# Softmax sums inverted on ten columns, the two halves of the attention output copied by ScalarE and added per head pair, and new numbers in the planner

## The chip, the cores and the metric

One core of a Trainium2 chip runs one program. Its engines are TensorE (PE; its weight loads are shown apart as PEld), VectorE (DVE), ScalarE (ACT), GpSimd (POOL) and SyncE (SP), which here only issues DMAs. The metric is the device time of one run in microseconds, from the first to the last instruction and what little lies around it.

## What is computed

Three layers in fp32, for 4 x 576 = 2304 tokens. Only the first is touched by the change.

```python
# attention: 4 batches, 8 heads, 576 positions, head size 64
scores = scale * q @ k.T + (cum[:, :, :, None] - cum[:, :, None, :])   # cum: running sum of log f
scores = where(causal, -1e9, scores); scores -= max(scores)
attn = exp(scores)
attn = attn / (sum(attn, axis=-1, keepdims=True) + 1e-09)
x = concat_heads(attn @ v)                                             # 2304 x 512
# first MLP
h = (x @ w1) * (x @ w2) @ w3;  x = h @ w_out
# second MLP
xn = x / rms(x) * rms_g;  y = (silu(xn @ w_gate) * (xn @ w_val)) @ w_out
```

## The kernel before

Most products run as three fp32r passes: a tensor is split into a rounded high part and the rest (two instructions: a copy with rounding and a subtraction), and high x high, high x low and low x high are added in PSUM.

**A planner sets all orders.** The program adds operations to a list with `plan.op([(engine, ns, lock), ...], ...)`. An operation can name several engines. `Plan.order()` then lays the operations out in time with the costs written in the code (`t_dve`, `t_act`, `t_pool`, `pe`), due times worked back from the dates that TensorE's operations carry (`S0`, `TE`, `T1`, `LT`, `LP`, `FD`, `FR`), the factor `WAIT`, and lags between engines that are longer in the middle of the program (`MARGIN`, `MARGIN2`). What it gives is the fixed order of each engine's queue, and the engine of each operation that had a choice. On the chip each engine works through its queue in order and waits for semaphores.

**Attention** takes 32 heads, two heads (p = 0, 1) to a pair. For one head: TensorE makes the scores (`attn_s`) in the PSUM tile `wide` and in two of the tiles `bank0` to `bank2`; DVE takes row maxima (`row_max`, L429, tiles `PB`, `nmax`); ACT makes the exponentials and their sums (`row_exp`, L436, `rsum`); TensorE transposes the blocks (L471); ACT and DVE split them (L486 `PTh`, L487 `PTl`); TensorE multiplies with V (`pv`, L520, L526) back into `wide`. V's high and low parts lie side by side as 128 columns, so that `wide` then holds two halves, partitions 0 to 63 and 64 to 127, whose sum is the head's output. In `pv` ACT copies the lower half to `half` (which lies in the tile `rq0`, L530) and DVE adds it to the upper half (L531) into the tile `x`; then `wide` is free for the next head's scores.

**The sums.** Once per pair TensorE transposes the 128 x 10 sums to 10 x 128 (L477), DVE adds 1e-9 (L478) and inverts (L479) that row tile `rrow`, and two DMAs spread it as `rall`. `normalize` multiplies `x` by `rall` (L536, DVE or POOL).

**Weights.** Beside the attention of the first heads, weights are loaded as integers and split: `convert` rescales their high words on ACT (L549) and their low words on DVE (L550), DVE joins the two (L552), and `unit` splits (L254, L256 the copies, L247 the subtractions). Then `wc_group` multiplies w3 by w_out (L625), so that the first MLP needs one product less. The first MLP (`ab_group` L662, `y_group` L687) runs between the later heads, the second (L867, L948) after them.

Of the kernel before, what the change touches and what calls it, by code (L numbers as in the profile page):

```python
# [51 lines left out]

S0, TE, T1 = 0, 7500, 13700
LT, LP = 5000, 13000

WC0, WCP = 18000, 9400

FD, FR = 25000, 1.8

WAIT, SLIP = 2.0, 1200  # L60

DMA0, COLD, RS, RB = 2500, 7000, 230, 330
MT, MARGIN, MARGIN2 = 135000, 600, 300
MT2, MARGIN3 = 538000, 200
# [148 lines left out]
def body(ctx, tc, q, k, v, f, w12, w3, wo1, wgv, wo2, g, out):  # L213
# [9 lines left out]
    def pe(cols, fn, r=(), w=(), at=0, times=1):  # L223

        plan.op([("PE", times * (max(110, 0.4167 * cols + 13.4)), False)], lambda e, times=times: fn(), r, w, at)

    def t_dve(n, rate=1.04, lock=False):
        return "DVE", 70 + rate * n, lock

    def t_act(n, fixed=95):  # L230
        return "ACT", fixed + 0.833 * n, False

    def t_pool(n, rate=2.1):
        return "POOL", 170 + rate * n, True
# [14 lines left out]
    def copy(n, o, a, r=(), w=(), by=1.0):  # L249

        def run(e):
            o_, a_ = (x() if callable(x) else x for x in (o, a))
            if e == "ACT":
                A.activation(o_, a_, AF.Copy, scale=by)  # L254
            else:
                on[e].tensor_scalar(out=o_, in0=a_, scalar1=by, scalar2=1.0, op0=ALU.mult, op1=ALU.mult)  # L256

        plan.op([t_act(n), t_dve(n, 0.52, True), t_pool(n, 0.83)], run, r, w)

# [30 lines left out]
    g_sb = const.tile([P, KD], F32, name="g_sb")  # L290
    tok = const.tile([P, 3 * BW // P], F32, name="tok")
    trow = const.tile([BW // P, P], F32, name="trow")

    rq = [att.tile([P, S], F32, name=f"rq{i}") for i in range(2)]
    half = rq[0][D:P, :]
    rk = [att.tile([P, S], F32, name=f"rk{i}") for i in range(2)]
# [164 lines left out]
    def transpose(h, parts, o, key, pt, at):  # L461
# [35 lines left out]
    def pv(h, at):  # L497
        p, j, (b, pp) = h % 2, h % 2, divmod(h // 2, H // 2)
        t, wk = wide, ["wide"]
# [28 lines left out]
        pe(192, tail, [(a, c) for a in ("PTh", "PTl") for c in (PT_KB0, PT_KB3)] + [("V2", p), ("V2h", p)], wk, at, 2)  # L528
        x_to, x_key = X[b % 2][j * D:(j + 1) * D, pp, :], ["cq"] * (b == 0) + wk + [("x", b % 2, pp, j)] + [("raw", "x1")] * (b == 1)
        act(S, lambda: A.copy(half, t[D:P, 0:S]), [], ["half", ("nrowq", 0)] + wk, at, 180)  # L530
        dve(S + 100, lambda: V.tensor_add(x_to, t[0:D, 0:S], half), ["half"], x_key, at)  # L531

    def normalize(h, at):
        b, pp = divmod(h // 2, H // 2)
        x = X[b % 2][:, pp, :]
        plan.op([t_dve(S, lock=True), t_pool(S)], lambda e: on[e].tensor_mul(x, x, rall), [("rall", 0), ("rall", 1)], [("x", b % 2, pp, j) for j in range(2)])  # L536

    def convert(raw, key, src, at_load, r_load=(), w_load=(), to=None):
# [4 lines left out]
        def lo():  # L543
            return u32(raw()).rearrange("p (n t) -> p n t", t=2)[:, :, 0]
# [494 lines left out]
    def start():  # L1039
# [179 lines left out]
```

## Time and profile before

| | |
|---|---|
| median of 3 runs | 952.07 us (950.26 to 952.71) |
| profiled execution | 951.07 us, its span 949.3 us |
| PE busy | 934.7 us, 98% of the span |
| DVE busy | 814.3 us, 86% |
| ACT busy | 516.1 us, 54% |
| POOL busy | 227.7 us, 24% |

The span runs from the first to the last instruction; 1.8 us of the execution lie around it. Busy times are averages over stages with different limits. A PE that is busy has matmuls in flight, which need not follow each other at full rate. TensorE's granted clock is 1.0 throughout, the level of 2.4 GHz.

### The profile page before, as it was taken

How to read it: one execution, taken by the hardware profiler on the slowest of the kernel's cores; microseconds unless marked ns; L12 is line 12 of the kernel's file. 1: busy time of each engine (PE TensorE's matmuls, PEld its weight loads, DVE VectorE, ACT ScalarE, POOL GpSimd, SP SyncE). 2: the span in 40 equal slices, each digit the busy share in tenths (PEclk: the TensorE clock that was granted, in tenths of full speed). 3: DMA queues.
4: the chain of work that ended last, by engine and by line, in shares of the span. 5: the costliest groups of instructions: out<-in, count | busy, mean ns of one | idle time of the engine just before them, and what ended most of it. 6: DMA issues, size and time to landing. Idle time of an engine off the chain costs nothing.

```text
span 949.3 us, 15520 instructions
## 1 busy us (share of the span) xinstructions
PE 934.7 (98%) x5516; PEld 894.5 (94%) x5516; DVE 814.3 (86%) x1486; ACT 516.1 (54%) x1056; POOL 227.7 (24%) x238
## 2 busy tenths in 40 slices
PE   8999999999999999999999999999999999999998
PEld 4687789999999999999999999999999999999998
DVE  8999999989997999475664779989988899988896
ACT  6777777757775567433332245446445456444442
POOL 2155326454445334202010021115000012000000
PEclk9999999999999999999999999999999999999999
DMA  6964565456545643166876335422754324633422
GB/s 229 294 214 162 159 218 180 167 197 208 188 149 185 196 147 134 30 256 244 300 247 235 112 117 196 175 105 68 228 210 141 106 91 147 223 137 117 134 68 100
DMA packets 47697, 161.67 MB, mean 170 GB/s; under 512 B 5674, under 2 KB 22236, under 8 KB 40964
## 3 DMA queue, kind: packets, MB, share of 16 engines
q1 hardware_dynamic: 47620, 160.69, 49.9%
q8 instruction: 43, 0.70, 0.3%
q14 instruction: 34, 0.28, 0.1%
HBM read 130.13 MB, written 30.53 MB: 169 GB/s over the span
## 4 chain that ended last, share of the span: by engine, by line
PE 73%; DVE 12%; DMA 2%; issue 2%; ACT 0%; SPq 0%; DVEq 0%
PE bank L867 27%; PE bank L662 16%; PE bank L687 10%; PE bank L948 9%; PE wide L948 3%; PE bank L471 3%; PE wide L520 3%; DVE PTl L487 1%; DVE wbig L247 1%; DMA raw_w<-in_wgv 1%; PE bank L625 1%; DVE qk L247 1%; PE bank L413 1%; PE bank L412 1%; DVE lbig L247 1%
## 5 line engine op out<-in xcount | busy, mean ns | idle before, releaser
L662 PE MATMUL bank<-xhl,wbig 128*128 128x384 f32 x1152 | 216.3, 338 | 0.1
L662 PEld LDWEIGHTS bank<-xhl,wbig 128*128 128x128 f32 x1152 | 198.0, 188 | 1.9 <-DVE xhl L247 0.4
L867 PE MATMUL bank<-xop,wbig 128*128 128x384 f32 x1008 | 182.3, 335 | 0.6 <-ACT cs L889 0.5
L867 PEld LDWEIGHTS bank<-xop,wbig 128*128 128x128 f32 x1008 | 175.1, 188 | 1.5 <-ACT cs L889 0.8
L867 PE MATMUL bank<-xop,lbig 128*128 128x384 f32 x504 | 94.4, 334 | 0.0
L867 PEld LDWEIGHTS bank<-xop,lbig 128*128 128x128 f32 x504 | 88.0, 188 | 0.0
L486 ACT CAST PTh<-bank 128x512 fp32r<-128x512 f32 (+2 forms) x116 | 55.3, 506 | 25.9 <-PE bank L471 21.5
L487 DVE TENSOR_TENSOR PTl<-bank,PTh 128x512 fp32r<-128x512 f32 (+2 forms) x116 | 64.3, 576 | 4.7 <-ACT PTh L486 4.4
L687 PE MATMUL bank<-uh,Wch 128*128 128x384 f32 x192 | 65.2, 339 | 0.0
L687 PE MATMUL bank<-uh,Wcl 128*128 128x384 f32 x192 | 64.3, 335 | 0.0
L687 PE MATMUL bank<-ul,Wch 128*128 128x384 f32 x192 | 64.2, 335 | 0.0
L625 PE MATMUL bank<-wbig,w 128*128 128x512 f32 x192 | 53.4, 406 | 0.5 <-DVE wbig L247 0.5
L670 ACT CAST uh<-u 128x384 fp32r<-128x384 f32 x48 | 24.6, 515 | 49.5 <-DVE u L669 49.4
L669 DVE TENSOR_TENSOR u<-bank,a 128x384 f32<-128x384 f32 x48 | 26.4, 550 | 29.1 <-PE bank L662 27.7
L520 PE MATMUL wide<-PTl,V 128*128 128x512 f32 (+4 forms) x145 | 43.6, 327 | 2.3 <-DVE PTl L487 2.2
L247 DVE TENSOR_TENSOR lbig<-zf,lbig 128x768 fp32r<-128x768 f32 x46 | 44.6, 976 | 0.1
L520 PE MATMUL wide<-PTh,V 128*128 128x512 f32 (+4 forms) x145 | 44.4, 317 | 0.1
L247 DVE TENSOR_TENSOR wbig<-nrm,wbig 128x768 fp32r<-128x768 f32 (+1 forms) x41 | 43.8, 1071 | 0.3 <-ACT wbig L254 0.3
L873 DVE TENSOR_TENSOR zf<-cs 128x384 f32<-128x384 f32 x72 | 40.1, 557 | 4.3 <-ACT cs L878 2.3
L765 POOL TENSOR_TENSOR xf<-xf 128x768 f32<-128x768 f32 (+1 forms) x5 | 23.8, 4756 | 81.7 <-DVE xf L552 25.4
L254 ACT ACTIVATE lbig<-zf 128x768 fp32r<-128x768 f32 x32 | 27.2, 850 | 25.7 <-PE bank L948 9.6
L625 PEld LDWEIGHTS bank<-wbig,w 128*128 128x128 f32 x192 | 33.9, 189 | 6.6 <-DVE wbig L247 1.2
(285 smaller groups left out, 2218.8 us busy)
## 6 DMA issues: line engine op xcount, KB each, us to landing
xf<-sw_d SPq DMA_DIRECT2D x24, 896.0 KB
nrm<-sw_d SPq DMA_DIRECT2D x12, 896.0 KB
wbig<-w_d SPq DMA_DIRECT2D x10, 1024.0 KB
rk<-in_k SPq DMA_DIRECT2D x62, 144.0 KB
nrm<-wo_d SPq DMA_DIRECT2D x11, 768.0 KB
raw_w<-in_wgv SPq DMA_DIRECT2D x8, 1024.0 KB
xf<-wo_d SPq DMA_DIRECT2D x10, 768.0 KB
sw_d<-raw_w SPq DMA_DIRECT2D x8, 896.0 KB
```

Source lines behind the costliest of these rows:

```text
L247: plan.op([t_dve(n, lock=True), t_pool(n)], lambda e: on[e].tensor_sub(*(x() if callable(x) else x for x in (o, a, b_))), r, w)
L254: A.activation(o_, a_, AF.Copy, scale=by)
L471: T.transpose(o[:, c * P:(c + 1) * P], PB[p][i][:, kb * P:(kb + 1) * P], ident)
L486: act(n, lambda: A.copy(PTh[:, pt:pt + n], o[:, lo:lo + n]), [], [("PTh", pt), key], at, 55)
L487: dve(n, lambda: V.tensor_sub(PTl[:, pt:pt + n], o[:, lo:lo + n], f32(PTh[:, pt:pt + n])), [("PTh", pt)], [("PTl", pt), key], at)
L520: pe(w, lambda s_=s_, o=o, w=w, c=c, kb=kb, m=m, src=src: T.matmul(t[:, o:o + w], V2[p][:, kb, :], src[:, c:c + w], start=(s_ == 0 and m = ...
L625: T.matmul(o, a, b_, start=(ft == 0 and m == 0), stop=(ft == KF - 1 and m == 2))
L662: T.matmul(o, a, x[:, kt, :], start=(kt == 0 and i == 0), stop=(kt == KD - 1 and i == 2))
L687: T.matmul(o, a[:, es], x[:, ft, 0:w], start=(q == 0 and ft % 2 == 0 and i == 0), stop=(q == 3 and ft % 2 == 1 and i == 2))
L867: T.matmul(o, w[:, a, j, kt], x[c][:, kt], start=start and kt == 0 and i == 0, stop=kt == 1 and i == 2, skip_group_check=not start)
L873: plan.op([t_dve(TH, lock=True), t_pool(TH)], lambda e: on[e].tensor_mul(o(), x(), y()), r, w)
L948: T.matmul(tiles[m], wv[:, a, k, m], z[c][:, kt], start=start and k == 0 and x == 0, stop=k == KH - 1 and x == 2, skip_group_check=not start)
```

## The change

Four edits go together.

1. **Sums.** 1e-9 is added and the inverse taken on the 128 x 10 tile `rsum`, ahead of the transpose. What follows the transpose is a plain copy to `rrow`, on ACT or DVE.
2. **Halves.** ACT copies both halves out of `wide`: the upper to `x`, the lower to a new tile `xlow`. Once per pair `normalize` adds `xlow` to `x` on 128 partitions, on DVE or POOL, and then multiplies.
3. **Low words.** `convert` may also rescale low words on ACT, as a Prelu with a slope of 0 and a bias column `under`.
4. **Numbers.** POOL's costs in the planner go up, and dates, lags and the factor `WAIT` change.

```diff
-S0, TE, T1 = 0, 7500, 13700
+S0, TE, T1 = 0, 8000, 13200
-FD, FR = 25000, 1.8
+FD, FR = 20000, 1.9
-WAIT, SLIP = 2.0, 1200
+WAIT, SLIP = 4.0, 1200
-MT, MARGIN, MARGIN2 = 135000, 600, 300
+MT, MARGIN, MARGIN2 = 135000, 600, 700
...
-    def t_pool(n, rate=2.1):
-        return "POOL", 170 + rate * n, True
+    def t_pool(n, rate=2.5):
+        return "POOL", 190 + rate * n, True
...
-        plan.op([t_act(n), t_dve(n, 0.52, True), t_pool(n, 0.83)], run, r, w)
+        plan.op([t_act(n), t_dve(n, 0.52, True), t_pool(n, 0.95)], run, r, w)
...
-            pe(128, lambda: T.transpose(row, rsum[pr].rearrange("p j i -> p (j i)"), ident), [("rsum", pr, j, i) for j in range(2) for i in range(5)], [key], at)
-            dve(P, lambda: V.tensor_scalar_add(rrow, row, 1.0e-9), [], ["rrow", key], at)
-            dve(P, lambda: V.reciprocal(rrow, rrow), [], ["rrow"], at)
+            dve(80, lambda: V.tensor_scalar_add(sums, sums, 1.0e-9), [], keys, at)
+            dve(100, lambda: V.reciprocal(sums, sums), [], keys, at)
+            pe(128, lambda: T.transpose(row, sums, ident), keys, [key], at)
+            plan.op([t_act(P), t_dve(P, 1.6)], lambda e: (A.copy if e == "ACT" else V.tensor_copy)(rrow, row), [], ["rrow", key])
...
-        act(S, lambda: A.copy(half, t[D:P, 0:S]), [], ["half", ("nrowq", 0)] + wk, at, 180)
-        dve(S + 100, lambda: V.tensor_add(x_to, t[0:D, 0:S], half), ["half"], x_key, at)
+        act(S, lambda: A.copy(x_to, t[0:D, 0:S]), [], x_key + wk, at)
+        act(S, lambda: A.copy(low, t[D:P, 0:S]), [], [("xlow", j)] + wk, at)
...
+        if h - 1 >= NP:
+            plan.op([t_dve(S, lock=True), t_pool(S)], lambda e: on[e].tensor_add(x, x, low), [("xlow", j) for j in range(2)], keys)
+        elif h >= NP:
+            dve(S, lambda: V.tensor_add(x[D:], x[D:], low[D:]), [("xlow", 1)], keys[1:])
+        plan.op([t_dve(S, lock=True), t_pool(S)], lambda e: on[e].tensor_mul(x, x, rall), [("rall", 0), ("rall", 1)], keys)
...
-        dve(1024, lambda: V.tensor_scalar(out=lo(), in0=lo(), scalar1=2.0**-29, scalar2=7.0, op0=ALU.mult, op1=ALU.min), [key], [kl], rate=0.52, lock=True)
+        def bits(e):
+            if e == "ACT":
+                A.activation(lo(), lo(), AF.Prelu, scale=2.0**-29, bias=under, alpha=0.0)
+            else:
+                V.tensor_scalar(out=lo(), in0=lo(), scalar1=2.0**-29, scalar2=7.0, op0=ALU.mult, op1=ALU.min)
+
+        plan.op([t_act(1024), t_dve(1024, 0.52, True)], bits, [key, "under"], [kl])
```

How this moves the queues is seen at three places.

DVE's queue in the second batch's first pairs, before: the row tile is made from the transposed sums (L478), and after a weight subtraction, a row maximum and three subtractions it is inverted on 128 columns (L479).

```order
L669 TENSOR_TENSOR u_133<-bank_64,a_131 128x384
L478 TENSOR_SCALAR rrow<-bank_60 10x128
L247 TENSOR_TENSOR wbig<-nrm,wbig 128x1024
L429 ISA PB4a,nmaxa<-wide,mask 128x576
L429 ISA nmaxa 128x1
L487 TENSOR_TENSOR PTl<-bank_59,PTh 128x448
L487 TENSOR_TENSOR PTl<-bank_60,PTh 128x320
L487 TENSOR_TENSOR PTl<-bank_61,PTh 128x384
L479 RECIPROCAL rrow<-rrow 10x128
```

And in the change, some ten rows earlier in the same heads' work: the sums are inverted on ten columns (L480, L481) among subtractions of the first MLP (`ul`), which stood on POOL before.

```order
L247 TENSOR_TENSOR qk_106<-rq_100,qk_106 64x576
L247 TENSOR_TENSOR qk_106<-rk_102,qk_106 64x576
L247 TENSOR_TENSOR wbig<-raw_w_1286,wbig 128x1024
L480 TENSOR_SCALAR rsumb<-rsumb 128x10
L247 TENSOR_TENSOR ul<-u_134,uh 128x384
L481 RECIPROCAL rsumb<-rsumb 128x10
L247 TENSOR_TENSOR wbig<-nrm,wbig 128x1024
L247 TENSOR_TENSOR ul<-u_135,uh 128x384
```

The inversion now stands ahead of the transpose that TensorE makes of the sums; the additions L531 are gone from this queue.

ACT's queue at the end of a head of the second batch, before: one copy out of `wide` (L530), other work behind it.

```order
L254 ACTIVATE wbig<-raw_w_1282 128x1024
L530 COPY rq_100<-wide 64x576
L667 COPY a_131<-bank_63 128x384
L254 ACTIVATE V_107<-rv_104 128x5x64
L254 ACTIVATE wbig<-nrm 128x1024
L486 CAST PTh<-bank_61 128x512
```

In the change, with a low-word pass (first row) and two copies out of `wide`; a weight copy and a split stand between the two.

```order
L563 ACTIVATE nrm<-nrm,tok 128x1024
L684 COPY a_132<-bank_62 128x384
L254 ACTIVATE wbig<-raw_ul 128x1024
L535 COPY x_131<-wide 64x576
L254 ACTIVATE wbig<-nrm 128x1024
L490 CAST PTh<-bank_61 128x512
L536 COPY xlow<-wide 64x576
```

`wide` is now given back by the second of these copies and not by DVE.

POOL's queue in the second batch, before: splits of V and of k, and the first MLP's subtractions `ul`.

```order
L247 TENSOR_TENSOR V_108<-rv_105,V_108 128x5x64
L256 TENSOR_SCALAR qk_106<-rk_102 128x576
L247 TENSOR_TENSOR qk_106<-rk_102,qk_106 64x576
L247 TENSOR_TENSOR ul<-u_133,uh 128x384
L247 TENSOR_TENSOR V_107<-rv_104,V_107 128x5x64
L247 TENSOR_TENSOR ul<-u_134,uh 128x384
```

In the change: the additions of pairs (L543) have come in, the subtractions of k and most of `ul` have gone to DVE.

```order
L543 TENSOR_TENSOR x_131<-x_131,xlow 128x576
L546 TENSOR_TENSOR x_131<-x_131,rall 128x576
L256 TENSOR_SCALAR qk_106<-rk_102 128x576
L247 TENSOR_TENSOR V_107<-rv_104,V_107 128x5x64
L256 TENSOR_SCALAR qk_106<-rk_103 128x576
L247 TENSOR_TENSOR qk_106<-rq_101,qk_106 64x576
```

Over the whole program POOL's queue holds 218 rows before and 162 in the change, DVE's 1438 and 1480, ACT's 878 and 931. TensorE has the same instructions in another order.

## Rows read from the trace of the kernel before

**Rows 1.** The page: span

```profile
span 949.3 us, 15520 instructions
```

**Rows 2.** Busy time by stretch: PE, PEld, DVE, ACT, POOL, clock, DMA share, GB/s

```profile
11.10:191.60 180.50, 173.38 (x992) 145.33 (x991) 177.29 (x374) 138.00 (x318) 77.86 (x80) 1.00 0.62 200
191.60:400.00 208.40, 207.19 (x1361) 201.41 (x1360) 178.95 (x409) 133.34 (x331) 86.86 (x99) 1.00 0.47 158
400.00:930.00 530.00, 529.36 (x3061) 527.74 (x3060) 438.81 (x674) 236.96 (x398) 59.80 (x37) 1.00 0.48 166
930.00:949.30 19.30, 15.82 (x92) 15.51 (x90) 10.95 (x17) 3.51 (x5) 0.00 (x0) 1.00 0.23 82
```

**Rows 3.** Waits of PEld, 11.1 to 191.6 us: total us, times, longest

```profile
PEld bank L471 <- DVE nmaxb L429: 2.9, 3, 1.4
PEld bank L471 <- DVE nmaxa L429: 2.9, 5, 0.9
PEld wide L520 <- DVE PTl L487: 2.3, 4, 1.0
PEld wide L510 <- ACT PTf L484: 1.9, 1, 1.9
...
PEld bank L625 <- DVE wbig L247: 1.2, 2, 0.8
```

**Rows 4.** Timeline of DVE near 102 us: start, us, what

```profile
101.65 0.94 DVE L479 RECIPROCAL rrow<-rrow 10x128 f32<-10x128 f32 x1
102.52 0.42 DVE L429 CUSTOM_DVE_ANT_0 PB2b<-bank,mask 128x320 f32<-128x320 f32 x1
...
103.99 0.75 DVE L531 TENSOR_TENSOR x<-wide,rq 64x576 f32<-64x576 f32 x1
```

**Rows 5.** Timeline of TensorE there, idle time before in brackets

```profile
103.87 0.33 PE L471 MATMUL bank<-ident,PB2a 128*128 128x128 f32 x1 [0.94 <-DVE nmaxb L429]
```

**Rows 6.** Groups of DVE, 11.1 to 191.6 us: busy us, mean ns, idle before

```profile
L531 DVE TENSOR_TENSOR x<-wide,rq 64x576 f32<-64x576 f32 x11 | 8.3, 750 | 0.3
L247 DVE TENSOR_TENSOR qk<-rk,qk 64x576 fp32r<-64x576 f32 x11 | 8.2, 741 | 0.2
L479 DVE RECIPROCAL rrow<-rrow 10x128 f32<-10x128 f32 x7 | 6.5, 933 | 0.0
L550 DVE TENSOR_SCALAR raw_ul<-raw_ul 128x1024 uint32<-128x1024 uint32 x4 | 2.7, 684 | 0.0
L478 DVE TENSOR_SCALAR rrow<-bank 10x128 f32<-10x128 f32 x7 | 1.9, 272 | 0.0
L247 DVE TENSOR_TENSOR w<-raw_ul,w 128x256 fp32r<-128x256 f32 x4 | 1.6, 408 | 0.0
L247 DVE TENSOR_TENSOR ul<-u,uh 128x384 fp32r<-128x384 f32 x1 | 0.5, 543 | 0.0
```

**Rows 7.** Groups of ACT, 11.1 to 191.6 us

```profile
L530 ACT COPY rq<-wide 64x576 f32<-64x576 f32 x11 | 7.0, 637 | 10.1 <-PE wide L526 10.1
L549 ACT ACTIVATE nrm<-nrm 128x1024 f32<-128x1024 f32 x6 | 6.9, 1154 | 1.6 <-DMA nrm<-in_w 1.6
```

**Rows 8.** Waits of ACT, 11.1 to 191.6 us

```profile
ACT PB3b L436 <- DVE nmaxb L429: 5.0, 5, 1.9
ACT PB2a L436 <- DVE nmaxa L429: 4.4, 4, 2.5
ACT PB2b L436 <- DVE nmaxb L429: 3.2, 2, 2.7
```

**Rows 9.** Single lines, whole span: count, min/median/max ns, first and last start

```profile
L531 DVE TENSOR_TENSOR x<-wide,rq x29: 748/750/752, 59.5 to 407.2; 64x576 f32<-64x576 f32 x29
L536 DVE TENSOR_TENSOR x<-x,rall x10: 740/746/1554, 112.3 to 408.2; 128x576 f32<-128x576 f32 x10
L536 POOL TENSOR_TENSOR x<-x,rall x6: 1407/1424/1622, 79.7 to 336.6; 128x576 f32<-128x576 f32 x6
L718 DVE SCALAR_TENSOR_TENSOR tok<-tok x18: 146/158/730, 241.7 to 565.1; 128x3 f32<-128x3 f32 x18
```

More of the change, by code (lines that the diff above doesn't have):

```diff
@@ L290, in body @@
     g_sb = const.tile([P, KD], F32, name="g_sb")
-    tok = const.tile([P, 3 * BW // P], F32, name="tok")
+    tok = const.tile([P, 3 * BW // P + 1], F32, name="tok")
+    under = tok[:, 3 * BW // P:]
     trow = const.tile([BW // P, P], F32, name="trow")
     rq = [att.tile([P, S], F32, name=f"rq{i}") for i in range(2)]
-    half = rq[0][D:P, :]
     rk = [att.tile([P, S], F32, name=f"rk{i}") for i in range(2)]
@@ L309, in body @@
     rall = att.tile([P, S], F32, name="rall")
+    xlow = att.tile([P, S], F32, name="xlow")
     mask = att.tile([P, S], F32, name="mask")
@@ L476, in transpose @@
             row, r_o = o[0:10, 3 * P:4 * P], r_d[h // 2]
-            pe(128, lambda: T.transpose(row, rsum[pr].rearrange("p j i -> p (j i)"), ident), [("rsum", pr, j, i) for j in range(2) for i in range(5)], [key], at)
-            dve(P, lambda: V.tensor_scalar_add(rrow, row, 1.0e-9), [], ["rrow", key], at)
-            dve(P, lambda: V.reciprocal(rrow, rrow), [], ["rrow"], at)
+            sums = rsum[pr].rearrange("p j i -> p (j i)")
+            keys = [("rsum", pr, j, i) for j in range(2) for i in range(5)]
+            dve(80, lambda: V.tensor_scalar_add(sums, sums, 1.0e-9), [], keys, at)
+            dve(100, lambda: V.reciprocal(sums, sums), [], keys, at)
+            pe(128, lambda: T.transpose(row, sums, ident), keys, [key], at)
+            plan.op([t_act(P), t_dve(P, 1.6)], lambda e: (A.copy if e == "ACT" else V.tensor_copy)(rrow, row), [], ["rrow", key])
             dma(5e3, lambda: SP.dma_start(out=r_o.rearrange("j (i n) -> (j i) n", i=5), in_=rrow), ["rrow"], [("rd", h // 2)])
@@ L497, in pv @@
     def pv(h, at):
-        p, j, (b, pp) = h % 2, h % 2, divmod(h // 2, H // 2)
+        p, j, pair, (b, pp) = h % 2, h % 2, h // 2, divmod(h // 2, H // 2)
         t, wk = wide, ["wide"]
@@ L528, in pv @@
         pe(192, tail, [(a, c) for a in ("PTh", "PTl") for c in (PT_KB0, PT_KB3)] + [("V2", p), ("V2h", p)], wk, at, 2)
-        x_to, x_key = X[b % 2][j * D:(j + 1) * D, pp, :], ["cq"] * (b == 0) + wk + [("x", b % 2, pp, j)] + [("raw", "x1")] * (b == 1)
-        act(S, lambda: A.copy(half, t[D:P, 0:S]), [], ["half", ("nrowq", 0)] + wk, at, 180)
-        dve(S + 100, lambda: V.tensor_add(x_to, t[0:D, 0:S], half), ["half"], x_key, at)
+        x_to, x_key = X[b % 2][j * D:(j + 1) * D, pp, :], ["cq"] * (b == 0) + [("x", b % 2, pp, j)] + [("raw", "x1")] * (b == 1)
+        low = xlow[j * D:(j + 1) * D, :]
+        act(S, lambda: A.copy(x_to, t[0:D, 0:S]), [], x_key + wk, at)
+        act(S, lambda: A.copy(low, t[D:P, 0:S]), [], [("xlow", j)] + wk, at)
     def normalize(h, at):
-        b, pp = divmod(h // 2, H // 2)
-        x = X[b % 2][:, pp, :]
-        plan.op([t_dve(S, lock=True), t_pool(S)], lambda e: on[e].tensor_mul(x, x, rall), [("rall", 0), ("rall", 1)], [("x", b % 2, pp, j) for j in range(2)])
+        pair, (b, pp) = h // 2, divmod(h // 2, H // 2)
+        x, low = X[b % 2][:, pp, :], xlow
+        keys = [("x", b % 2, pp, j) for j in range(2)]
+        if h - 1 >= NP:
[3 more added lines that the diff above has]
+        plan.op([t_dve(S, lock=True), t_pool(S)], lambda e: on[e].tensor_mul(x, x, rall), [("rall", 0), ("rall", 1)], keys)
     def convert(raw, key, src, at_load, r_load=(), w_load=(), to=None):
@@ L1053, in start @@
         dve(70, lambda: V.memset(rows_c, 1.0), w=["picks"])
+        dve(70, lambda: V.memset(under, -0.501), w=["under"])
         act(1500, lambda: A.activation(rows_c[:, 0:1], rows_c[:, 0:1], AF.Ln), [], ["picks"])
```

## Prediction

> **What bounds the kernel now.** The first view is the busy time by stretch [rows 2]. From 191.6 us on TensorE is hardly ever idle: 1.2 us of 208.4, then 0.6 us of 530. DVE has 86% and 83% there, ACT less, so nothing that another engine saves there can shorten the time by more than those 1.8 us; the 3.5 us at the very end are the last copies and stores. The stretch from 11.1 to 191.6 us is another matter (it runs from the first head's row maximum of block 4 to the sixteenth head's). DVE is busy for 177.3 of its 180.5 us, and TensorE sits idle for 7.1 us. That is the least that TensorE loses there, because a matmul that ends late still counts as busy.
>
> The second view, the waits of PEld, shows who it waits for: the four rows that name DVE (row maxima, low halves of the transposed blocks, weight splits) come to 2.9 + 2.9 + 2.3 + 1.2 = 9.3 us, and one wait on ACT is 1.9 us [rows 3]. The third view, the timeline, shows how: the inversion of a pair's sums starts at 101.65 us, the row maximum PB2b stands behind it in DVE's queue and starts at 102.52 [rows 4], and TensorE, waiting for that head's maxima, had stood still for 0.94 us when it went on at 103.87 [rows 5]. So in this stretch a microsecond less on DVE is about a microsecond less of the time, until TensorE's idle time is used up.
>
> **The change, part by part.** All counts are taken in the order of each queue between those two row maxima, before and after. A DVE instruction overlaps the next by some 0.07 us (0.94 us long, a step of 0.87 [rows 4]); I leave that out except for the inversion.
>
> *Sums.* Seven pairs lose the inversion (step 0.87 [rows 4]) and the addition (0.27 [rows 6]): 7 x 1.14 = 8.0 us. They gain two instructions on ten columns. Nothing in the trace has ten columns; the nearest row below is three columns, 0.16 us [rows 9], the bound above is 0.27 us for an inversion scaled from 128 columns with that fixed part (0.16 + 10/128 of 0.93 = 0.23) and for the addition as it was. I take 0.16 each: 2.2 us. The copy to the row tile falls on DVE three times (0.27 as the addition that read the same row from PSUM [rows 6], 0.8 us) and on ACT four times. Saved on DVE: 5.0 us; with the upper bounds 3.7.
>
> *Halves.* 11 additions of 0.75 us go from DVE [rows 6]: 8.3 us. Three pair additions come back in this stretch, one of them on 64 partitions, at 0.75 us each by the product of the same shape [rows 9]: 2.2 us; three more go to POOL at 1.42 us [rows 9]. Saved: 6.0 us. If each met a busy POOL, as the longest of those products seems to have done at 1.55 us [rows 9], they would cost 2.4 us more.
>
> *Low words.* Eight of the passes leave DVE, 0.68 us each [rows 6]: 5.5 us.
>
> *What the planner moves back.* With POOL dearer in its costs, POOL's queue has 61 instead of 82 vector instructions up to the first square of the first MLP's output. Six more subtractions `ul` fall on DVE at 0.54 us, three of k at 0.74, seven of w3 at 0.41 [rows 6]: 3.3 + 2.2 + 2.9 = 8.4 us. The other moves cancel: V's splits, q's and some copies come, k's and the weights' high parts go, each 0.3 to 1.3 us. I take 0 for them, with 1 us to either side.
>
> DVE's sum: 5.0 + 6.0 + 5.5 - 8.4 = 8 us less of 177. By bounds it is 3.4 to 9 us (3.7 for the sums, 3.6 for the halves, 5.5 for the low words, 9.4 given back; or the values taken with 7.4 given back).
>
> *ACT pays.* 11 more copies at 0.64 us, eight low-word passes at 1.15 us as its high-word passes [rows 7], four short copies (between nothing and 0.64 us each, I take 0.25, since they have 128 columns and not 576), and by the planner six more copies of k and q less four of V, about 2.2 us: 7.0 + 9.2 + 1.0 + 2.2 = 19.4 us. ACT goes from 138.0 to 157.4 us in this stretch [rows 2]. That is hidden as long as its work is ready when its turn comes; the rival below prices the other case.
>
> *`wide`.* It used to be free after ACT's copy and DVE's addition, which waited for its turn: in the head shown the addition starts at 103.99, behind two row maxima and two more instructions [rows 4]. Now a second copy on ACT frees it, behind whatever ACT's order puts between. I count nothing for it either way; the addition that is gone took 0.75 us and its queue, the copy takes 0.64 and ACT's.
>
> *A new wait.* TensorE's transpose of the sums now follows DVE's inversion. Behind it in TensorE's queue stand the other transposes or weight products. Sixteen times at most the 0.3 us of the two short instructions: 5 us if DVE were always the last, 0 if never. In the stretch it is seven times; I take 0.5 us.
>
> *Later stretches.* DVE takes over more of POOL's work there (42 more instructions over the whole program). From 400 us on DVE has 91 us of idle time in 530 [rows 2], which hides it; some of the splits at the changes of a token block are waited for, up to 2 us if that cover is gone.
>
> Sum: 8 us on DVE, of which TensorE can use its 7.1 us of idle time and something of what it loses inside busy time; less 0.5 us for the transposes: 7.5 us. The profiled execution took 951.07 us, 1.8 us more than its span of 949.3 [rows 1]; it becomes 943.6. The median of the runs is 952.07, 1.0 above the profiled one, so I forecast **944.5 us**, and for this case alone 940 to 949.
>
> **The rivals.**
>
> *ACT takes the place of DVE.* In the stretch ACT has 42.5 us in which it waits (180.5 - 138.0 [rows 2]). With 157.4 us of work, the stretch gets shorter only if these waits fall under 23 us, and the kernel is slower by over 0.3% (2.9 us) if they stay over 26. For it: exponentials, block splits and now the freeing of `wide` all queue in order behind 1.15 us passes. Against it: 10.1 us of the waits are for the product with V [rows 7] and 12.6 for row maxima [rows 8], that is for a DVE that was late, and they shrink with its load. At 30 us of waits the time is 952.1 + 6.9 = 959 us. Chance 0.14.
>
> *Nothing gained.* The same with waits of 20 to 26 us, or DVE's 8 us lost again to waits for ACT: 950 to 954 us. Chance 0.13.
>
> *More than DVE's sum.* TensorE gets back all four DVE rows of its waits, 9.3 us, and the later `wide` rows as the earlier freeing lets scores start sooner: 12 us, 940 us. For it: POOL's instructions, a quarter fewer, hold up DVE less. Against: DVE at 169 of some 170 us is still close to the bound. Chance 0.13.
>
> *Additions that meet POOL.* The addition L531 read one operand from PSUM and one from SBUF and took 748 to 752 ns in all 29 cases, while POOL was busy or not; the product of two SBUF tensors took 740 to 1554 ns [rows 9]. The pair additions are of the second kind. If such waits cost each DVE one 0.8 us (2.4 us in the stretch), the gain is 5 us: 947 us. Chance 0.08. The Trainium skill, "SBUF — State Buffer", section "Who interferes with whom", says that a DVE instruction with two SBUF inputs and a GpSimd instruction that reads SBUF exclude each other, the second waiting for the first to end, while one with a single SBUF input does not contend; the two ranges of durations here agree with that, and it speaks against this part of the change.
>
> **How the numbers follow.** The forecast has 0.52, with more (0.13) and the additions that meet POOL (0.08) the faster side has 0.73; no change 0.13; slower 0.14. About 0.3%, 2.9 us, is what a measurement of this kernel can tell from no change. The range runs from 938, a little under the case of more, to 955, the upper end of nothing gained; it leaves out most of the slower rival.
>
> **What would show it.** Right: the same stretch, from row maximum to row maximum, is 6 to 9 us shorter, DVE still nearly full in it, ACT at some 155 us, and TensorE's waits on row maxima about halved. The ten-column instructions show at 0.15 to 0.25 us. Wrong: ACT's row over 165 us or its waits not shrunk; TensorE waiting for exponentials or for `PTh`; a wait at the transpose of the sums that names the inversion; pair additions of 1.5 us; or idle time of TensorE after 400 us of more than 2 us, which would mean that POOL's work was hidden and is not any more on DVE.

## The result, and the profile after

The change takes 943.33 us (median of 4 runs, 942.71 to 943.71) against 951.48 for the kernel before beside it: a ratio of 0.9914, 95% interval 0.9896 to 0.9931, so it is 8.1 us faster. The profiled execution took 943.71 us. The page of the change, span and busy times, where [rows 1] had 949.3 us:

```profile
span 941.9 us, 15490 instructions
...
PE 930.3 (99%) x5516; PEld 897.2 (95%) x5516; DVE 803.8 (85%) x1540; ACT 545.0 (58%) x1105; POOL 140.3 (15%) x167
```

Busy time by stretch of the change, columns as in [rows 2]. The first row runs from the first head's row maximum of block 4 to the sixteenth head's (11.15 to 191.56 us before); the next three go on to the end of the span, and the others are parts of these:

```profile
11.98:185.68 173.70, 170.31 (x995) 147.91 (x994) 165.57 (x379) 156.80 (x346) 54.45 (x60) 0.99 0.65 210
185.68:400.00 214.32, 213.09 (x1393) 207.45 (x1392) 182.24 (x450) 144.55 (x354) 55.45 (x58) 1.00 0.48 156
400.00:923.00 523.00, 523.00 (x3029) 522.63 (x3028) 437.29 (x679) 235.71 (x396) 27.22 (x27) 1.00 0.49 166
923.00:941.90 18.90, 15.03 (x87) 14.71 (x85) 10.16 (x16) 2.84 (x5) 0.00 (x0) 0.97 0.23 84
...
20.00:30.00 10.00, 7.91 (x38) 5.61 (x37) 9.53 (x21) 8.94 (x19) 1.11 (x1) 0.83 0.99 302
...
110.00:135.00 25.00, 25.00 (x149) 22.65 (x148) 23.45 (x50) 22.89 (x44) 9.25 (x10) 1.00 0.82 258
135.00:160.00 25.00, 25.00 (x165) 24.53 (x164) 24.26 (x52) 22.89 (x55) 10.18 (x7) 1.00 0.56 183
160.00:185.00 25.00, 25.00 (x168) 24.45 (x168) 22.64 (x52) 20.85 (x51) 4.97 (x5) 1.00 0.58 193
...
600.00:930.00 330.00, 330.00 (x1906) 330.00 (x1905) 300.20 (x423) 163.08 (x271) 2.68 (x3) 1.00 0.40 136
```

The span is 7.4 us shorter: 6.7 in the stretch (180.4 to 173.7), 1.5 behind it, less 0.8 that the stretch begins later. In the stretch TensorE's idle time fell from 7.1 to 3.4 us, DVE's busy time from 177.2 to 165.6, POOL's from 77.8 to 54.5, and ACT's rose from 137.9 to 156.8. From 110 to 185 us TensorE is never idle, so DVE's idle time there costs nothing. The same stretches before, where DVE was full and TensorE idle in the first and the third (the last row belongs to a later reading):

```profile
110.00:135.00 25.00, 24.49 (x135) 20.34 (x134) 24.76 (x43) 16.74 (x36) 6.78 (x6) 1.00 0.81 262
135.00:160.00 25.00, 25.00 (x164) 24.44 (x163) 24.84 (x50) 22.32 (x48) 13.65 (x10) 1.00 0.45 147
160.00:185.00 25.00, 23.85 (x150) 22.31 (x150) 24.78 (x49) 17.26 (x43) 12.04 (x11) 1.00 0.51 178
...
600.00:930.00 330.00, 329.36 (x1896) 328.22 (x1896) 300.28 (x414) 164.90 (x274) 30.41 (x9) 1.00 0.42 140
```

Waits of PEld in the stretch of the change (total us, times, longest), to set beside [rows 3]:

```profile
PEld bank L472 <- POOL wbig L256: 2.3, 1, 2.3
...
PEld wide L514 <- ACT rows_c L1097: 1.3, 1, 1.3
...
PEld wide L514 <- DVE nmaxa L430: 0.7, 1, 0.7
...
PEld bank L472 <- DVE nmaxb L430: 0.3, 1, 0.3
```

The two waits of the transposes for row maxima, 5.8 us before, have shrunk to the 0.3 us of the last row. DVE's groups in the stretch (busy us, mean ns of one, idle before):

```profile
L247 DVE TENSOR_TENSOR qk<-rk,qk 64x576 fp32r<-64x576 f32 x14 | 11.0, 786 | 0.3
L247 DVE TENSOR_TENSOR ul<-u,uh 128x384 fp32r<-128x384 f32 x7 | 4.5, 642 | 0.0
L543 DVE TENSOR_TENSOR x<-x,xlow 128x576 f32<-128x576 f32 x2 | 1.5, 754 | 0.2 <-ACT xlow L536 0.2
L483 DVE COPY rrow<-bank 10x128 f32<-10x128 f32 x3 | 0.8, 272 | 0.0
L481 DVE RECIPROCAL rsuma<-rsuma 128x10 f32<-128x10 f32 x4 | 0.8, 204 | 0.0
L565 DVE TENSOR_SCALAR raw_ul<-raw_ul 128x1024 uint32<-128x1024 uint32 x1 | 0.7, 711 | 0.0
```

ACT's groups in the stretch, for [rows 7], and its largest waits, for [rows 8]:

```profile
L536 ACT COPY xlow<-wide 64x576 f32<-64x576 f32 x11 | 7.0, 636 | 0.2
L535 ACT COPY x<-wide 64x576 f32<-64x576 f32 x11 | 7.0, 634 | 3.5 <-PE wide L530 3.3
L563 ACT ACTIVATE raw_ul<-raw_ul,tok 128x1024 uint32<-128x1024 uint32 x3 | 3.8, 1280 | 0.0
```

```profile
ACT x L535 <- PE wide L530: 3.3, 2, 2.1
ACT PTh L490 <- PE wide L530: 2.9, 2, 1.5
...
```

Single lines over the whole span (count, min/median/max ns, first and last start):

```profile
L480 DVE TENSOR_SCALAR rsuma<-rsuma x8: 156/158/418, 27.2 to 357.0; 128x10 f32<-128x10 f32 x8
...
L481 DVE RECIPROCAL rsuma<-rsuma x8: 201/206/216, 28.4 to 357.5; 128x10 f32<-128x10 f32 x8
...
L543 DVE TENSOR_TENSOR x<-x,xlow x11: 744/749/1130, 83.7 to 394.3; 128x576 f32<-128x576 f32 x11
...
L545 DVE TENSOR_TENSOR x<-x,xlow x1: 1767/1767/1767, 67.5 to 67.5; 64x576 f32<-64x576 f32 x1
...
L247 DVE TENSOR_TENSOR qk<-rq,qk x27: 751/752/1879, 23.8 to 367.5; 64x576 fp32r<-64x576 f32 x27
```

The new instructions lie inside their bounds (0.16 to 0.27 us). Subtractions of q take 0.75 us, but up to 1.88 at times: such an excess over the usual length is called "held up" below.

### The profile page after: what moved, and what is told of

Same layout as the page of the kernel before. It is cut to its first block, busy times and chain, and to the rows that moved or that the text cites. A ratio compares the mean times of both kernels' runs of the same rounds, so it can differ in the third digit from the quotient of the medians.

```text
span 941.9 us, 15490 instructions
## 1 busy us (share of the span) xinstructions
PE 930.3 (99%) x5516; PEld 897.2 (95%) x5516; DVE 803.8 (85%) x1540; ACT 545.0 (58%) x1105; POOL 140.3 (15%) x167
## 4 chain that ended last, share of the span: by engine, by line
PE 91%; DVE 6%; ACT 2%; issue 1%; DVEq 0%; ACTq 0%
PE bank L884 28%; PE bank L679 21%; PE bank L965 10%; PE bank L704 10%; PE bank L472 5%; PE wide L524 4%; PE wide L965 4%; PE bank L642 3%; PE bank L414 1%; PE bank L413 1%; DVE qk L247 1%; DVE PTl L491 1%; PE wide L514 1%; PE wide L530 1%; PE wide L413 1%
## 5 line engine op out<-in xcount | busy, mean ns | idle before, releaser
L884 PE MATMUL bank<-xop,wbig 128*128 128x384 f32 x1008 | 181.8, 334 | 0.0
L491 DVE TENSOR_TENSOR PTl<-bank,PTh 128x512 fp32r<-128x512 f32 (+3 forms) x116 | 64.2, 580 | 4.3 <-ACT PTh L490 4.2
L490 ACT CAST PTh<-bank 128x512 fp32r<-128x512 f32 (+3 forms) x116 | 54.8, 504 | 12.8 <-PE wide L530 6.0
L906 ACT COPY cs<-bank 128x384 f32<-128x384 f32 x36 | 17.3, 481 | 43.0 <-PE bank L884 43.0
L535 ACT COPY x<-wide 64x576 f32<-64x576 f32 x29 | 18.4, 633 | 38.2 <-PE wide L530 38.1
L254 ACT ACTIVATE lbig<-zf 128x768 fp32r<-128x768 f32 x27 | 23.0, 850 | 29.3 <-PE bank L965 11.0
```

Source lines behind the costliest of these rows:

```text
L490: act(n, lambda: A.copy(PTh[:, pt:pt + n], o[:, lo:lo + n]), [], [("PTh", pt), key], at, 55)
L491: dve(n, lambda: V.tensor_sub(PTl[:, pt:pt + n], o[:, lo:lo + n], f32(PTh[:, pt:pt + n])), [("PTh", pt)], [("PTl", pt), key], at)
L884: T.matmul(o, w[:, a, j, kt], x[c][:, kt], start=start and kt == 0 and i == 0, stop=kt == 1 and i == 2, skip_group_check=not start)
```

## The experiments

**Theory D** is the prediction's: the gain is DVE's work in the stretch, and the time moves with it. From f1 on it has a second term, what DVE is held up. **Theory A**: ACT, with 157 us of work, is the new bound. **Theory W**: the gain comes from `wide` being given back by ACT. **Theory N**: the new numbers make the gain, not the work taken off DVE. Later runs split N into **P** (POOL's costs) and **T** (dates, lags, `WAIT`), and look at an early wait (**E**) and at chance in the planner's order (**L**).

The table splits the stretch of each profiled execution, from the first to the sixteenth head's row maximum. Held up is summed over DVE's instructions of the stretch: how far each exceeds the quick quarter of the same shapes, where that is over 60 ns. Own work is busy time less held up. Own work, held up and idle add up to the stretch in every run, so the sum itself tests nothing; what tests a theory is which of them an edit moves and whether the time follows. The split is of the one profiled execution, whose time stands beside it and can lie some us from the median. The addition on 64 partitions (L545 in the change) is the only one of its shape in a run, so what it is held up stands under own work: 1.0 us in the change, e7 and g1 (there read 1.0 less own work and 1.0 more held up), 0.4 in e1, under 0.2 in the others.

| run | median us | ratio to before, 95% | profiled us | stretch | DVE own work | held up | idle | ACT busy |
|---|---|---|---|---|---|---|---|---|
| before | 951.48 | | 951.07 | 180.4 | 168.7 | 8.5 | 3.2 | 137.9 |
| the change | 943.33 | 0.9914 (0.9896–0.9931) | 943.71 | 173.7 | 162.1 | 3.5 | 8.1 | 156.8 |
| e1_sums_back | 948.88 | 0.9977 (0.9968–0.9987) | 950.96 | 181.2 | 169.9 | 3.5 | 7.8 | 149.1 |
| e2_halves_back | 943.25 | 0.9916 (0.9902–0.9930) | 943.63 | 174.5 | 162.7 | 6.7 | 5.1 | 149.6 |
| e3_low_on_dve | 945.04 | 0.9929 (0.9917–0.9942) | 943.31 | 174.2 | 162.8 | 5.6 | 5.8 | 144.7 |
| e4_numbers_back | 949.77 | 0.9983 (0.9974–0.9992) | 951.11 | 181.5 | 163.9 | 10.2 | 7.4 | 148.8 |
| f1_sums_only | 948.97 | 0.9976 (0.9966–0.9987) | 948.88 | 178.2 | 164.8 | 9.4 | 4.0 | 139.6 |
| f4_numbers_only | 947.77 | 0.9955 (0.9942–0.9968) | 948.29 | 181.8 | 173.1 | 4.7 | 4.0 | 144.1 |
| e7_pair_add_dve | 944.83 | 0.9924 (0.9909–0.9938) | 945.39 | 176.5 | 164.1 | 6.7 | 5.7 | 154.5 |
| g6_ptf_act | 944.33 | 0.9921 (0.9907–0.9935) | 944.83 | 176.7 | 160.3 | 6.3 | 10.1 | 154.5 |
| e5_pool_costs_back | 949.21 | 0.9975 (0.9965–0.9985) | 948.14 | 177.8 | 163.6 | 9.7 | 4.5 | 153.1 |
| e6_dates_back | 943.78 | 0.9926 (0.9911–0.9942) | 947.50 | 179.5 | 162.7 | 10.3 | 6.5 | 153.5 |
| g1_dates_near | 943.57 | 0.9928 (0.9915–0.9940) | 943.00 | 174.8 | 162.6 | 7.7 | 4.5 | 153.6 |
| g4_wait_back | 939.62 | 0.9880 (0.9868–0.9893) | 940.77 | 172.2 | 159.7 | 7.7 | 4.8 | 153.4 |

Each ratio is to the kernel before run beside it (medians of 951.19 to 951.48 us).

### e1_sums_back: the change without the edit on the sums

```diff
-            dve(80, lambda: V.tensor_scalar_add(sums, sums, 1.0e-9), [], keys, at)
-            dve(100, lambda: V.reciprocal(sums, sums), [], keys, at)
-            pe(128, lambda: T.transpose(row, sums, ident), keys, [key], at)
-            plan.op([t_act(P), t_dve(P, 1.6)], ...(rrow, row), [], ["rrow", key])
+            pe(128, lambda: T.transpose(row, rsum[pr]..., ident), ..., [key], at)
+            dve(P, lambda: V.tensor_scalar_add(rrow, row, 1.0e-9), [], ["rrow", key], at)
+            dve(P, lambda: V.reciprocal(rrow, rrow), [], ["rrow"], at)
```

> The change with the sums as before (transposed first, then 1e-9 added and inverted on 128 columns by DVE). Theory D (the gain is DVE's work in the first 190 us): by the order, DVE has 172 us of work between the first and the sixteenth head's row maxima, 10 us more than in the change (5 us for the inversions, the rest is work that the planner then moves to DVE), so the gain of 8 us is gone: 949 to 953 us. Theory W (the gain is the tile wide, which two copies of ACT now free sooner): the inversion matters only by its own length, at most 5 us: 944 to 948 us. Theory L (the gain is luck of the order): any time within 5 us of 943.

Measured 948.88 us: 5.5 us of the gain are gone, and in the profiled execution, 2.1 us above the median, the stretch is back at its old length. Its busy times, columns as above, and TensorE's waits for row maxima in it, which the change had all but ended:

```profile
11.98:193.21 181.23, 172.73 (x992) 146.54 (x991) 173.41 (x383) 149.11 (x329) 55.59 (x65) 0.99 0.62 200
```

```profile
PEld bank L472 <- DVE nmaxb L430: 3.2, 5, 1.1
...
PEld bank L472 <- DVE nmaxa L430: 2.2, 2, 1.8
```

ACT has 8 us less to do than in the change and the stretch is 7.5 us longer, along with DVE's own work (+7.8, some 5 of it the longer instructions by what was expected, the rest work that the planner moved to DVE). That speaks for D, whose range it misses by 0.1 us, and against A.

### e2_halves_back: the change with the old end of a head

```diff
-        act(S, lambda: A.copy(x_to, t[0:D, 0:S]), [], x_key + wk, at)
-        act(S, lambda: A.copy(low, t[D:P, 0:S]), [], [("xlow", j)] + wk, at)
+        act(S, lambda: A.copy(half, t[D:P, 0:S]), [], ["half", ("nrowq", 0)] + wk, at, 180)
+        dve(S + 100, lambda: V.tensor_add(x_to, t[0:D, 0:S], half), ["half"], x_key, at)
```

and without the addition of pairs in `normalize`.

> The change with the halves as before (ACT copies one half, DVE adds from PSUM for each head). The planner answers by leaving more to POOL, so that DVE's work up to the sixteenth head's row maximum is the same as in the change (161.7 against 161.9 us) while ACT has 7 us less and POOL 10 us more. Theory D: no change, 942 to 945 us, or up to 2 us more where POOL and DVE hold each other up. Theory W: wide is again freed by a DVE instruction that waits for its turn, 947 to 951 us. Theory A (ACT is the new bound in the first 60 us): faster, 938 to 941 us.

Measured 943.25 us, the time of the change. W falls: with `wide` given back by DVE again nothing is lost. Nor do 11 more additions lengthen DVE's own work, because the planner answers: POOL does 78 instructions in the stretch instead of 60.

```profile
11.98:186.47 174.49, 171.29 (x991) 146.86 (x990) 169.42 (x369) 149.61 (x333) 70.97 (x78) 0.99 0.63 208
```

DVE is held up 3.2 us more by the table and idle 3.0 us less. So a saving on DVE counts only as far as the planner cannot get the same from POOL, and a microsecond held up need not cost one where DVE would else sit idle.

### e3_low_on_dve: low words on DVE alone

```diff
-        plan.op([t_act(1024), t_dve(1024, 0.52, True)], bits, [key, "under"], [kl])
+        plan.op([t_dve(1024, 0.52, True)], bits, [key, "under"], [kl])
```

> The change with all low words on DVE. DVE has 2.7 us more than the change up to the sixteenth head's row maximum (the planner gives some other work to ACT and POOL), ACT 12 us less. Theory D: 945 to 948 us. Theory W: no change, 942 to 944. Theory A (ACT is the new bound early): faster, 938 to 941 us.

Measured 945.04 us, 1.7 us above the change with 12 us less on ACT. A falls again, since a lighter ACT brings nothing. For D it shows little: the intervals of the two ratios overlap, and the 1.7 us go with TensorE's clock. Two runs at the full granted clock took 942.70 and 943.31 us, as the change does; the three at 0.996 took 945.04 to 945.65.

### e4_numbers_back: the three work edits with the old numbers

```diff
-S0, TE, T1 = 0, 8000, 13200
+S0, TE, T1 = 0, 7500, 13700
-FD, FR = 20000, 1.9
+FD, FR = 25000, 1.8
-WAIT, SLIP = 4.0, 1200
+WAIT, SLIP = 2.0, 1200
-MT, MARGIN, MARGIN2 = 135000, 600, 700
+MT, MARGIN, MARGIN2 = 135000, 600, 300
-    def t_pool(n, rate=2.5):
+    def t_pool(n, rate=2.1):
-        return "POOL", 190 + rate * n, True
+        return "POOL", 170 + rate * n, True
```

and 0.83 for 0.95 in POOL's copy.

> The change with all the planner's numbers as before (POOL's costs, dates, WAIT, MARGIN2); the three edits of the work stay. DVE has 3.5 us more up to the sixteenth head's row maximum than the change, POOL some 5 us more in that stretch and 37 us more in the whole program. Theory D: 946 to 948 us. Theory N (the new numbers spare DVE waits for POOL, late in the program too, where the last 350 us lost 2.3 us before and 0.6 us after): 947 to 950 us. Theory L: within 5 us of 943 either way.

Measured 949.77 us: without the new numbers the three edits bring 1.4 us. That lies outside D's range and inside N's. DVE's own work stays almost as low as in the change (163.9), but it is held up 10.2 us instead of 3.5. So D needs its second term, which the prediction had left out of its sum.

### f1_sums_only and f4_numbers_only: one part alone, in the kernel before

`f1` is the kernel before with the new lines on the sums, `f4` the kernel before with the new numbers (the diff of e1 and of e4, turned round).

> The kernel before with the sums edit alone (inverted on ten columns ahead of the transpose). DVE's work up to the sixteenth head's row maximum falls from 170.4 to 165.5 us, POOL's instructions stay. Theory D (the first 190 us go with DVE's work plus what POOL holds it up plus its idle time): 3 to 5 us faster than before, 946 to 948 us. Theory N (the edits of the work bring little as long as the planner's numbers let POOL hold DVE up, as the run with the numbers back showed): within 2 us of before, 949 to 951 us.

> The kernel before with the planner's new numbers alone. DVE's own work up to the sixteenth head's row maximum rises from 170.4 to 174.4 us, as POOL hands work back. Theory D with the hold-ups by POOL: 4 us of work more and about 5 us of hold-ups less in the first 190 us, and 1.6 us less lost after 600 us: 948 to 951 us. If the numbers alone are what made the change faster: 943 to 946 us. If own work is all that counts: 954 us.

Measured 948.97 and 947.77 us: 2.5 and 3.7 us faster than before. `f1` misses the 3 to 5 us of D and comes out at the edge of N's range; `f4` is 0.2 us under D's. The sums alone take 3.9 us off DVE's own work, and the stretch shortens by 2.2. The numbers alone lengthen the stretch by 1.4 us, as DVE gets 4.4 us of POOL's work and is held up 3.8 us less; their gain lies elsewhere, since TensorE has done 1007 matmuls in that stretch instead of 992, and late in the program (no idle time from 600 to 930 us, as in the change). The numbers' 3.7 and the 1.4 of e4 make 5.1 of 8.1 us: 3 us come only when both are there.

### e7_pair_add_dve: the additions of pairs on DVE alone

```diff
-            plan.op([t_dve(S, lock=True), t_pool(S)], ...tensor_add(x, x, low), ...)
+            plan.op([t_dve(S, lock=True)], ...tensor_add(x, x, low), ...)
```

> The change with all pair additions on DVE (three in the first stretch were on POOL). DVE has 1.7 us more up to the sixteenth head's row maximum. Theory D: 944 to 946 us. If additions of two SBUF tensors on DVE meet POOL often (0.8 us each for 13 of them): 949 to 954 us. If POOL's slow additions are what holds DVE up: 940 to 942 us.

Measured 944.83 us, 1.5 us slower than the change, with 2.0 us more of own work. As D has it, though the intervals of the two ratios overlap.

### g6_ptf_act: copies of the first heads' transposed blocks on ACT alone

TensorE's timeline in the change, early (start us, us, what, idle time before in brackets):

```profile
20.05 0.27 PE L472 MATMUL bank<-ident,PB3a 128*128 128x128 f32 x1
20.16 0.27 PE L472 MATMUL bank<-ident,PB4a 128*128 128x128 f32 x1
22.52 0.30 PE L472 MATMUL bank<-ident,PB3a 128*128 128x128 f32 x1 [2.09 <-DVE PTf L488]
...
23.25 0.42 PE L472 MATMUL bank<-ident,PB1a 128*128 128x128 f32 x1
23.46 0.42 PE L472 MATMUL bank<-ident,PB2a 128*128 128x128 f32 x1
```

TensorE stands still for 2.09 us for a copy on DVE, and then its transposes step 0.21 us instead of 0.11, as at the lower of its two levels, 1.2 GHz; the granted clock of 20 to 30 us is 0.83 on the mean. The run gives those copies to ACT.

```diff
-            plan.op([t_act(n, 55), t_dve(n)], ...(PTf()...)
+            plan.op([t_act(n, 55)], ...(PTf()...)
```

> The change, with the copies of the first three heads' transposed blocks (PTf) offered to ACT alone. In the change TensorE stands still for 2.1 us at 20 us, waiting for such a copy in DVE's queue behind a weight pass and two row maxima, and its granted clock is 0.83 between 20 and 30 us. Theory E (that wait and the low clock cost the change 2 to 4 us early): no such wait, 939 to 942 us. Theory D alone: DVE has 0.5 us less, ACT 2 us less by what else moves: 942 to 943.5 us. If ACT is full early, 944 to 946 us.

Measured 944.33 us, no gain. It lies in the range that was named for an ACT full early: from 30 to 40 us ACT is busy for all of 10.00 us (9.54 in the change) and TensorE idles 1.4 us there (0.2). The clock stays at 1.00, but between 20 and 30 us TensorE idles 2.4 us for other reasons (2.1 in the change):

```profile
20.00:30.00 10.00, 7.60 (x45) 5.57 (x44) 9.94 (x25) 9.13 (x21) 1.13 (x1) 1.00 0.93 313
```

E falls as a cost that this edit gives back: the wait went elsewhere.

### e5_pool_costs_back and e6_dates_back: the numbers in two halves

`e5` is the change with POOL's three old costs, `e6` the change with the old dates, lags and `WAIT` (the two halves of e4's diff).

> The change with POOL's costs in the planner as before; the new dates, WAIT and MARGIN2 stay. DVE has 3.2 us more work of its own up to the sixteenth head's row maximum than the change, POOL 29 us more in the whole program. Theory P (the numbers help because POOL, priced as it really is, holds DVE up less, early and late): 947 to 950 us, with over 6 us of DVE held up in the first 190 us and about 2 us lost by TensorE after 600 us. Theory T (the numbers help by their dates, which bring more of TensorE's work beside the early heads): 943 to 945 us.

> The change with the dates, WAIT and MARGIN2 as before; POOL's new costs stay. DVE has 1.3 us more than the change up to the sixteenth head's row maximum. Theory P: 943 to 946 us, little lost after 600 us. Theory T: 947 to 950 us.

Measured 949.21 and 943.78 us. P holds: without POOL's new costs 5.9 us are lost, and without the new dates, lags and `WAIT` together nothing that can be measured (the table's split of e6 is of a profiled execution of 947.5 us, with a granted clock of 0.68 from 20 to 30 us, so its median is the number to use). With the old costs TensorE waits for DVE again, as the waits of PEld in e5's stretch show:

```profile
PEld wide L524 <- DVE PTl L491: 2.8, 3, 1.8
PEld bank L472 <- POOL wbig L256: 2.3, 1, 2.3
PEld bank L472 <- DVE nmaxa L430: 2.0, 4, 0.9
...
PEld bank L472 <- DVE nmaxb L430: 1.4, 2, 1.1
```

DVE is held up 6.2 us more than in the change and has 1.5 us more of own work by the table (5.3 and 2.3 with the 64-partition additions read as held up). One of its subtractions, 0.75 us as a rule, took 2.81, and late in the program TensorE loses 2.2 us, where the change loses none:

```profile
L247 DVE TENSOR_TENSOR qk<-rq,qk x28: 751/753/2809, 25.1 to 368.6; 64x576 fp32r<-64x576 f32 x28
```

```profile
400.00:930.00 530.00, 527.76 (x3044) 525.15 (x3044) 440.98 (x675) 236.68 (x397) 52.94 (x34) 1.00 0.48 164
```

So the 5.9 us are lost in two places, early on DVE and late.

### g1_dates_near and g4_wait_back: other numbers nearby

```diff
-S0, TE, T1 = 0, 8000, 13200
+S0, TE, T1 = 0, 8100, 13250
```

> The change with two dates moved by a hair (TE 8100 for 8000, T1 13250 for 13200), which does not change what the work is but lets the planner lay out another order. Theory D: DVE has 0.6 us more up to the sixteenth head's row maximum, 943 to 945 us. Theory L (the order's luck is as large as the edits): more than 2.5 us away from 943.3 either way.

Measured 943.57 us. Slightly shifted dates give another order and the same time. The other runs say the same more widely: the eight orders that have both the edit on the sums and POOL's new costs (the change, e2, e3, e6, e7, g1, g4, g6) take 939.62 to 945.04 us, the five that lack one of the two (e1, e4, e5, f1, f4) 947.77 to 949.77. So the 8 us are no chance of one order; a chance of some us remains inside each group. A kernel with these two parts alone was not run.

```diff
-WAIT, SLIP = 4.0, 1200
+WAIT, SLIP = 2.0, 1200
```

> The change with WAIT at 2 as before and everything else new. Of the orders tried DVE has the least work up to the sixteenth head's row maximum, 160.1 us, 1.8 us less than the change (with 4.4 us more of it ahead of the second head's row maximum), ACT 1 us less, POOL as much. Theory D: 940.5 to 943 us, faster than the change. Theory L: within 3 us of 943 either way.

Measured 939.62 us, 3.7 us under the change (3.1 under its run at the full granted clock, which all four runs here had) and 11.7 under the kernel before: the best version here, and under the ranges of both D and L. Its stretch:

```profile
11.25:183.49 172.24, 168.53 (x987) 145.18 (x986) 167.41 (x379) 153.44 (x339) 60.35 (x63) 1.00 0.65 212
```

It begins 0.7 us earlier and is 1.5 us shorter, with 2.4 us less of DVE's own work and 3.3 less idle, against 4.2 more held up; 0.7 us more come behind it. Whether `WAIT` does this as such, or this one order is lucky, stays open: with the same `WAIT` and the other old dates, e6 stands at 943.78. So the nothing of e6 can hide two parts that cancel: with `WAIT` at 2 the other new dates and lags are worth 4.2 us, and putting `WAIT` to 4, as the change does, takes 3.7 of it back.

## Why the prediction was right

**The place and the size.** The forecast was 944.5 us and a span of 941.8; measured were 943.33 and 941.9. The stretch became 6.7 us shorter, within the 6 to 9 that were named, and undoing the sums (e1) brought TensorE's waits for row maxima back, as a bound on DVE would, while unloading ACT (e2, e3) gained nothing.

**The terms of DVE's sum**, measured as the time from each instruction to the next in its queue (us, taken off DVE):

| term | predicted | measured |
|---|---|---|
| sums | 5.0 | 7.5 - 2.2 = 5.3 |
| halves | 6.0 | 8.3 - 3.2 = 5.1 |
| low words | 5.5 | 5.4 |
| moved back from POOL (`ul`, k, w3) | -8.4 | -3.6 - 2.6 - 1.0 = -7.2 |
| all the rest of DVE's busy time | 0 | 3.0 |
| sum | 8 | 11.6 |

The single terms hold within about 1 us (eight low words at 0.68 us are 5.4 and not 5.5). The halves came out 1 us smaller because of the addition of 1.77 us (below). The inversion on ten columns takes 0.206 us, not 0.16, but the next instruction mostly starts 0.13 us after it. The step that was mis-sized is the rest, counted at nothing: the sum left out that a less busy POOL holds DVE up less. Of the rest's instructions the held-up time alone fell from 6.5 to 2.1 us. By the table above own work fell by 6.6 us and held-up time by 5.0 in all (7.6 and 4.0 with the addition of 1.77 us read as held up). That was the argument of the rival *more than DVE's sum*, given 0.13. Of the 11.6 us less on DVE the stretch got only 6.7, because DVE's idle time grew by 4.9 us: from 110 to 185 us TensorE is full, and DVE can give no more there. TensorE's side was mis-sized too: of its 7.1 us of idle time it could use 3.7, and the other 3.0 came from inside busy time, for which the forecast had "something". So the mechanism, a stretch bound by DVE's queue, was right; that the size fits to within 1.2 us is in part luck, since a saving left out and idle time left out nearly cancelled.

**Which edit it was.** The forecast credited the gain to the work edits, with the planner's moves as a price of 8.4 us. The runs show it otherwise. Taken out of the change, all the numbers cost 6.4 us (e4), POOL's costs 5.9 (e5), the three work edits together 4.4 (f4). Put into the kernel before, the numbers bring 3.7 us (f4), the work edits 1.4 (e4), the sums alone 2.5 (f1). So the numbers count for more either way. Among the work edits it is the sums: halves (6.0 us in the forecast's sum) can be undone at no loss (e2), low words (5.5) at 1.7 us or less (e3), as the planner finds the same elsewhere. The total came out near since the order of the queues was counted with all four edits in.

**ACT** was to have 157.4 us and has 156.8, its low words at 1.22 to 1.35 us instead of 1.15. Its waits fell from 42.5 to 16.9 us, under the 23 that decided that rival; the waits for row maxima, 12.6 us in [rows 8], are gone from the top of its list.

**Additions that meet POOL.** It happened once in the stretch: the addition on 64 partitions took 1.77 us where its like takes 0.75 [rows 9]; the others take 0.75, and one later 1.13. That is 1 us, not 2.4. DVE's and POOL's timelines at that place; POOL's product ends at 68.64 us, and DVE's addition 0.62 us later:

```profile
67.49 1.77 DVE L545 TENSOR_TENSOR x<-x,xlow 64x576 f32<-64x576 f32 x1
```

```profile
67.20 1.44 POOL L546 TENSOR_TENSOR x<-x,rall 128x576 f32<-128x576 f32 x1
```

**The transposes' wait**, taken at 0.5 us, did not occur: no transpose of the sums waited for the inversion. (One matmul of the scores waited 0.4 us, by the profile for the addition L480.)

**Later stretches** were counted as hidden, with up to 2 us at risk. From 600 to 930 us TensorE lost its last 0.6 us of idle time and did ten more matmuls: a small gain where only a loss was considered. It goes with POOL's 30.4 us of work there before and 2.7 after, and is no matter of windows that lie differently in a shorter program: e1, which takes nearly as long as the kernel before, has no idle time of TensorE from 400 to 930 us either, and 3071 matmuls where that has 3061.

## What to carry to other kernels

A planner's cost for a slow helper engine has to include what that engine holds up on the one that is the bound. The old cost of POOL's instruction on 128 x 576 was 1.38 us in the code (170 + 2.1 x 576 ns) and fits what it takes undisturbed, 1.42 [rows 9]; the new one, 1.63, is above it, and undoing that rise cost more here than undoing three edits that shortened DVE's work. Undo each part alone before crediting it, since a planner (like a scheduler) can answer an undone edit elsewhere (e2) or make two parts worth more together than apart; and undo a group of numbers one by one too, since they can cancel (e6 and g4). A saving on a full engine pays up to the point where the next engine is full; look in the windows for where that is, stretch by stretch.

## What the runs showed that was not expected

In the kernel before, late in the program, subtractions on POOL took many times what the same shape takes on DVE. POOL's timeline and its group from 600 us on:

```profile
645.95 13.34 POOL L765 TENSOR_TENSOR xf<-xf 128x768 f32<-128x768 f32 x1 [9.30 <-ACT lbig L254]
```

```profile
L765 POOL TENSOR_TENSOR xf<-xf 128x768 f32<-128x768 f32 x3 | 21.9, 7291 | 46.6 <-DVE xop L247 25.3 <-PE bank L867 12.0 <-ACT lbig L254 9.3
```

and DVE's timeline as that subtraction ends, at 659.29 us:

```profile
655.76 0.95 DVE L247 TENSOR_TENSOR lbig<-zf,lbig 128x768 fp32r<-128x768 f32 x1
656.62 0.95 DVE L765 TENSOR_TENSOR zf<-zf 128x768 f32<-128x768 f32 x1
657.59 2.11 DVE L256 TENSOR_SCALAR wbig<-zf 128x768 fp32r<-128x768 f32 x1
659.62 0.55 DVE L256 TENSOR_SCALAR lbig<-zf 128x768 fp32r<-128x768 f32 x1
```

While DVE runs subtraction after subtraction, POOL's lasts 13.3 us; when it gets through, a DVE copy that takes 0.55 us next time takes 2.11. So each engine can hold up the other.

The traces show how far this explains the table's held-up time. In the stretches of all 14 profiled executions 209 of DVE's 5313 instructions are more than 60 ns over their usual length. Each of the 209 began while a POOL instruction was running that ended before it did, and 207 of them end a fixed time after that POOL instruction: 0.10 to 0.16 us less than their own usual length, as if they had started when POOL was done. None of the 209 reads a bank or `wide` in PSUM, although 2135 of the 5313 do and POOL was running at the start of 995 of those; the held-up ones read SBUF alone, and 127 of them are subtractions, additions or products of two SBUF tensors. So the held-up time is DVE waiting for POOL's instruction to end.

The mean granted clock differs a little between runs of one kernel. Runs of the change with 1.000, 0.999 and 0.998 took 942.71, 943.23 and 943.42 to 943.71 us; in e2 they took 941.93, 942.86 and 943.63 to 943.99; the one run of e6 with 0.996 took 947.5, and the runs of e3 differ likewise (above). In the profiled executions of the change and of e6 the low clock lies between 20 and 30 us (0.83 and 0.68), in the change right behind the stop of 2.09 us. Times differ at one clock too (942.65 to 945.11 us among the runs of e6 at 1.000), so this is a tendency of 1 to 2 us here and no measured price.
